# Adding a block-diagonal residual with 64-row matmuls in pairs instead of 128-row matmuls

## The chip, the cores and the metric

The kernel runs on 1 core of one Trainium2 chip. The metric is the device time of one execution in microseconds (us). The five engines are named as the profile names them: PE is TensorE (PE for its matmuls, PEld for its weight loads), DVE is VectorE, ACT is ScalarE, POOL is GpSimd and SP is SyncE.

## What is computed

Attention packs 576 tokens into 32 (`p` attends to `k` and `v`), the tokens then read from the packed ones (`q` attends to the packed result), and a mixer follows: a low-rank mix over tokens, a residual `u`, and a two-layer network with a second residual.

```
p_packed = sm_attn(p, k, v)                  # 8 batches, 8 heads of 64 columns
x        = sm_attn(q, p_packed, p_packed)    # heads side by side: [8, 576, 512]
h = x.T @ U @ V                              # low rank, over tokens
u = x + h.T
out = u + relu(u @ w_ch1) @ w_ch2            # 512 -> 2048 -> 512
```

## The kernel before

`x` is never formed. It is a matrix of attention weights times the packed values, so `u` of one batch is also a matrix of adjusted weights (256 packed rows per token) times a block-diagonal matrix of packed values. The kernel keeps the adjusted weights, transposed, as two parts `ah` and `al` (high and low half of the number, each in fp32r): 128 partitions, two groups `g` of 4 heads, and 576 tokens. In a group the 128 partitions hold 4 heads of 32 packed rows each. The block-diagonal values are `rh` and `rl` (the trace calls both batches' tiles `rdh` and `rdl`): 128 partitions, two groups, 4 heads, 64 columns. Partition block x of group g has values only in the columns of head `x ^ g`, and zeros elsewhere. A product of two split numbers is three matmuls, `mm3` (lines 86 to 88): high by high, high by low, low by high.

A batch goes through 16 steps `kt`, each of 128 of the 2048 hidden columns. `gemm1(kt)` makes hidden columns in two halves of 320 and 256 tokens into `h_ps`, ACT and DVE apply the relu and split the result into `hh` and `hl`, and `gemm2(kt - 1)` of the step before adds 128x512 products into four open accumulators `o[0..3]`, one for each 128 tokens, one PSUM bank each. The remaining 64 tokens of a batch are handled for two batches together by `joint`, which also uses `residual`. Between `gemm1` and `gemm2`, and behind `gemm2`, stand single steps of the next batch's attention (`steps`) and, where `kt % 4 == 2`, `fold`, which multiplies packed values by the first layer's weights. The order of the instructions is the order of this loop, written out by hand.

At `kt == 1` `blocks` fills `rh` and `rl` for the batch. At `kt == 3` `add_u` adds the residual to the four open accumulators: for each token tile t and each group g, `mm3` with a 128x128 stationary tile of `ah` or `al` and 256 moving columns of `rh` or `rl`. This is 4 x 2 x 3 = 24 matmuls in a batch.

```
        def add_u(self):
            for t in range(4):
                c0 = 5 * I * (t // 2) + P * (t % 2)
                ts_ = slice(c0, c0 + P)
                residual(self.o[t], self.ah[:, :, ts_], self.al[:, :, ts_], self.rh, self.rl)
```

Other lines that the trace names: line 229 is `scores` (64x32 stationary tiles at eight places of the array), line 361 is `fold` (64x32 as well), line 304 is `mix1` (128x128 stationary, 256 fp32r columns, and for the last 64 tokens 64x128), lines 318 and 321 are `mix2` (fp32r, 256 and 64 columns).

Of the kernel before, what the change touches and what calls it, by code (L numbers as in the profile page):

```python
# [19 lines left out]
def packed_attention_mixer_kernel(  # L20
# [27 lines left out]
    nc = tc.nc  # L48
# [5 lines left out]
    P = 128  # L54
    SM = 512
    NT = 9
    I = S // NT
# [26 lines left out]
    def mm3(ps, lhs, rhs, start, stop):  # L84
        (lh, ll), (rh, rl) = lhs, rhs
        nc.tensor.matmul(ps, lhsT=lh, rhs=rh, start=start, stop=False)  # L86
        nc.tensor.matmul(ps, lhsT=lh, rhs=rl, start=False, stop=False)  # L87
        nc.tensor.matmul(ps, lhsT=ll, rhs=rh, start=False, stop=stop)  # L88
# [27 lines left out]
    def w2_tiles(pool, n):  # L116
        for i in range(n, n + 2):
            w2t[i] = tuple(pool.tile([P, 4, DM], F32R, name=f"w2{x}{i}", tag=f"w2{x}{i}", bufs=1) for x in "hl")
# [30 lines left out]
    def load_w2(kt):  # L149
        b = bits["w2", kt] = bits_tile()  # L150
        nc.sync.dma_start(out=b.rearrange("p x t -> p (x t)"), in_=w2[kt * P:(kt + 1) * P, :])

    def convert_w2(kt):
        return kt, float32_of(conv_tile(I32), conv_tile(F32), bits.pop(("w2", kt)))

    def split_w2(kt, x):
        hi, lo = w2_parts(kt)
        nc.scalar.copy(hi, x)
        nc.gpsimd.tensor_tensor(lo, x, hi.bitcast(F32), op=ALU.subtract)
# [196 lines left out]
    def fold(b, c):  # L356
        f_ps = [bank() for _ in range(2)]
        for h in range(H):
            g, z = h // 4, h % 2
            xs, zs = slice(32 * (h % 4 ^ g), 32 * (h % 4 ^ g) + 32), slice(64 * z, 64 * z + 64)  # L360
            nc.tensor.matmul(f_ps[g][xs], lhsT=ppT[b][zs, g, xs], rhs=w1t[h // 2][zs, QW * c:QW * c + QW],  # L361
                             start=True, stop=True)
        for a in range(2):
            hi, lo = (pipe.tile([P, 2, QW // 2], F32R, name=f"wt{x}", tag=f"wt{x}", bufs=3) for x in "hl")
            cs = slice(QW // 2 * a, QW // 2 * a + QW // 2)
            for g in range(2):
                nc.scalar.copy(hi[:, g], f_ps[g][:, cs])  # L367
                nc.vector.tensor_tensor(lo[:, g], f_ps[g][:, cs], hi[:, g].bitcast(F32), op=ALU.subtract)  # L368
            wt[b, 2 * c + a] = hi, lo
# [192 lines left out]
    class Batch:  # L562
# [44 lines left out]
                ts_ = slice(t * P, t * P + P)  # L607
                mm3(self.o[t], (hh[:, ts_], hl[:, ts_]), w2_parts(kt), kt == 0, kt == NK - 1)

        def add_u(self):  # L610
            for t in range(4):
                c0 = 5 * I * (t // 2) + P * (t % 2)
                ts_ = slice(c0, c0 + P)
                residual(self.o[t], self.ah[:, :, ts_], self.al[:, :, ts_], self.rh, self.rl)

        def store(self):
            for j in range(2):
# [8 lines left out]
    def residual(ot, xh, xl, rh, rl):  # L626
        for g in range(2):
            mm3(ot[:, g * 256:(g + 1) * 256], (xh[:, g], xl[:, g]), (rh[:, g], rl[:, g]), False, False)

    def joint_parts(b, n):  # L630

        hi, lo = conv_tile(F32R), conv_tile(F32R)
        k0 = 4 * n
        for (dst, src) in ((slice(0, 1), jslot(b, k0)), (slice(1, 4), k0 + 1)):
            w = dst.stop - dst.start
            src = hj[:, src:src + w].rearrange("p k x -> p (k x)")
            cs = slice(P * dst.start, P * dst.stop)
            nc.scalar.copy(hi[:, cs], src)
            nc.vector.tensor_tensor(lo[:, cs], src, hi[:, cs].bitcast(F32), op=ALU.subtract)
        return hi, lo  # L640

    def joint(b, parts):

        oj = psO.tile([P, DM], F32, name="o", tag="o")
        for kt in range(NK):
            if kt % 4 == 0:
                hi, lo = parts.pop(0)
                if kt // 4 + 2 < NK // 4:
                    parts.append(joint_parts(b, kt // 4 + 2))
            cs = slice(P * (kt % 4), P * (kt % 4) + P)  # L650
            mm3(oj, (hi[:, cs], lo[:, cs]), w2_parts(kt), kt == 0, kt == NK - 1)
            if kt == 0:
                for i in range(2):
                    residual(oj, ajh[i], ajl[i], rdh[i], rdl[i])
        return oj

    def store_joint(b, oj):
        os_ = conv_tile(F32)
        nc.scalar.copy(os_, oj)
        for i in range(2):  # L660
            nc.sync.dma_start(out=out[b - 1 + i].rearrange("(i c) m -> c i m", c=NT)[8], in_=os_[I * i:I * i + I])

    w2x = convert_w2(1)
    last, parts = None, []
    for b in range(B):
        cur = Batch(b)
        oj = None
        ahead = attention(b + 2, res) if b + 2 < B else []
        for kt in range(NK):
            cur.gemm1(kt)  # L670
            if oj and kt == 1:
                store_joint(b - 1, oj)
            if rest:
                rest.pop(0)()
            elif steps and (b == 0 or kt % 4 != 2):
                steps.pop(0)()
            if (b, kt) == (0, 5):
                w2_tiles(ctx.enter_context(tc.tile_pool(name="sC", bufs=1, side="right", reuse_waits="tile")), 2)
            if kt > 0:
                cur.gemm2(kt - 1)  # L680
            elif last:
                last.gemm2(NK - 1)
                last.store()
                if last.b % 2 == 1:
                    oj = joint(last.b, parts)
            if w2x:
                split_w2(*w2x)
                w2x = None
                if kt + 3 < NK:
                    load_w2(kt + 3)  # L690
                if kt + 2 < NK:
                    w2x = convert_w2(kt + 2)
            if kt % 4 == 2 and (b, kt) != (B - 1, NK - 2):
                n = b * NPC + kt // 4 + 1
                fold(n // NPC, n % NPC)
            elif steps:
                steps.pop(0)()
            if kt == 1:
                cur.blocks()
            if kt == 3:  # L700
                cur.add_u()
            if ahead and kt == 13:
                ahead.pop(0)()
            if kt == NK - 1 and b % 2 == 1:
                parts = [joint_parts(b, 0), joint_parts(b, 1)]
        assert not steps
        steps = ahead
        last = cur
# [35 lines left out]
```

## Time and profile before

| | us |
|---|---|
| median of 3 runs | 881.36 (880.0 to 882.8) |
| profiled execution, its own time | 877.17 |
| profiled execution, span from first to last instruction | 875.2 |
| PE busy | 836.0 (96% of the span) |
| PE weight loads busy | 665.1 (76%) |
| DVE busy | 402.6 (46%) |
| ACT busy | 322.8 (37%) |

The first 122 us pack the tokens. From there the eight batches follow each other. The mean granted clock of TensorE over the span is 0.973 of full speed. A row of the view of instructions in order of time gives the start, the recorded duration and the instruction. Recorded durations of matmuls overlap, since they are pipelined: what a matmul costs in a dense stream is the distance from its start to the start of the next one.

### The profile page before, as it was taken

What the parts mean: (1) busy time and instruction counts of PE and PEld (TensorE: products, weight loads), DVE (VectorE), ACT (ScalarE), POOL (GpSimd) and SP (SyncE); (2) the same over time, 40 slices, a digit from 0 to 9 for tenths busy, and PEclk for the clock granted to TensorE, in tenths of its full rate; (3) what the DMA queues carried; (4) which work ended last, traced back from release to release, by engine and by line L of the source; (5) the groups of instructions that cost most, each with busy time, mean ns of one, the idle gap of its engine ahead of it and who ended that gap; (6) DMA issues with size and microseconds to landing.
All of it is one profiled execution on the core that took longest, in us unless ns stands there. A gap on an engine that the chain in (4) does not pass through costs nothing.

```text
span 875.2 us, 14665 instructions
## 1 busy us (share of the span) xinstructions
PE 836.0 (96%) x5808; PEld 665.1 (76%) x5808; DVE 402.6 (46%) x988; ACT 322.8 (37%) x1000; POOL 95.0 (11%) x111
## 2 busy tenths in 40 slices
PE   5878899979999999999999999999999999999997
PEld 2554557858888888788878878888888887888886
DVE  4699757876433323433443433434343334332221
ACT  3666564534322333234223332233223332332221
POOL 0002222323001100100010000110011001010000
PEclk8799799989999999999999999999999999999999
DMA  8999833322100110011001100011001100010001
GB/s 273 290 337 292 278 115 102 95 75 85 49 1 1 61 53 10 1 61 49 1 1 61 49 13 1 1 61 49 1 1 61 48 13 1 1 49 1 1 1 60
DMA packets 38979, 59.08 MB, mean 68 GB/s; under 512 B 11776, under 2 KB 21888, under 8 KB 38912
## 3 DMA queue, kind: packets, MB, share of 16 engines
q1 hardware_dynamic: 38912, 58.16, 20.4%
q8 instruction: 45, 0.74, 0.4%
q14 instruction: 22, 0.18, 0.1%
HBM read 47.79 MB, written 10.35 MB: 66 GB/s over the span
## 4 chain that ended last, share of the span: by engine, by line
PE 85%; DVE 7%; DMA 4%; issue 1%; ACT 1%; POOL 0%; SPq 0%; ACTq 0%; DVEq 0%; POOLq 0%
PE o L86 16%; PE o L88 16%; PE o L87 16%; PE h_ps L86 8%; PE h_ps L88 7%; PE h_ps L87 7%; PE t_ps L361 4%; DMA bits<-in_moe_w_ch_dram 2%; PE t_ps L208 1%; DVE os L80 1%; PE t_ps L229 1%; PE s_ps L229 1%; PE t_ps L304 1%; PE t_ps L236 1%; DMA x<-in_moe_U_dram 1%
## 5 line engine op out<-in xcount | busy, mean ns | idle before, releaser
L86 PE MATMUL o<-w2h,hh 128*128 128x512 f32 x512 | 208.7, 408 | 0.0
L88 PE MATMUL o<-w2h,hl 128*128 128x512 f32 x512 | 203.5, 397 | 0.0
L87 PE MATMUL o<-w2l,hh 128*128 128x512 f32 x512 | 203.0, 397 | 0.0
L599 DVE SCALAR_TENSOR_TENSOR hl<-h_ps,hh 128x256 fp32r<-128x256 f32 x256 | 104.4, 422 | 167.2 <-ACT hj L598 154.4
L596 ACT ACTIVATE hh<-h_ps 128x256 fp32r<-128x256 f32 x256 | 98.9, 388 | 188.9 <-PE h_ps L88 188.1
L86 PE MATMUL h_ps<-ah,wth 128*128 128x320 f32 (+1 forms) x512 | 158.2, 309 | 1.2 <-DVE hl L599 1.2
L87 PE MATMUL h_ps<-al,wth 128*128 128x320 f32 (+1 forms) x512 | 151.6, 296 | 0.0
L88 PE MATMUL h_ps<-ah,wtl 128*128 128x320 f32 (+1 forms) x512 | 151.4, 296 | 0.0
L86 PEld LDWEIGHTS h_ps<-ah,wth 128*128 128x128 f32 x512 | 96.9, 189 | 32.7 <-issue 25.7
L88 PEld LDWEIGHTS o<-w2h,hl 128*128 128x128 f32 x512 | 97.1, 190 | 23.1
L86 PEld LDWEIGHTS o<-w2h,hh 128*128 128x128 f32 x512 | 97.4, 190 | 22.2 <-issue 4.1
L87 PEld LDWEIGHTS o<-w2l,hh 128*128 128x128 f32 x512 | 97.6, 191 | 17.4
L87 PEld LDWEIGHTS h_ps<-al,wth 128*128 128x128 f32 x512 | 97.0, 189 | 1.9
L88 PEld LDWEIGHTS h_ps<-ah,wtl 128*128 128x128 f32 x512 | 97.0, 190 | 0.0
L368 DVE TENSOR_TENSOR wtl<-t_ps,wth 128x256 fp32r<-128x256 f32 x128 | 48.5, 419 | 93.9 <-ACT wth L367 90.5
L367 ACT CAST wth<-t_ps 128x256 fp32r<-128x256 f32 x128 | 43.4, 374 | 109.1 <-PE t_ps L361 97.1
L324 POOL TENSOR_TENSOR al<-aT,ah 128x320 fp32r<-128x320 f32 (+1 forms) x32 | 26.2, 818 | 211.6 <-ACT ah L323 211.6
L268 POOL TENSOR_TENSOR e<-e,m 128x576 f32<-128x576 f32 x16 | 19.6, 1226 | 237.8 <-DVE m L267 232.4
L361 PE MATMUL t_ps<-w1t,ppT 64*32 64x512 f32 x512 | 36.5, 601 | 0.0
L323 ACT CAST ah<-aT 128x320 fp32r<-128x320 f32 (+1 forms) x32 | 13.9, 433 | 52.8 <-DVE aT L322 52.8
L279 POOL TENSOR_TENSOR e<-e,s 128x576 f32<-128x576 f32 x16 | 18.9, 1179 | 110.3 <-DVE s L278 106.4
L296 DVE TENSOR_TENSOR x<-t_ps,x 128x512 fp32r<-128x512 f32 (+1 forms) x24 | 14.3, 599 | 32.6 <-ACT x L295 32.6
(130 smaller groups left out, 1021.9 us busy)
## 6 DMA issues: line engine op xcount, KB each, us to landing
bits<-in_moe_w_ch_dram SPq DMA_DIRECT2D x32, 512.0 KB, 4.9
kx<-in_k_dram SPq DMA_DIRECT2D x16, 576.0 KB, 6.1
x<-in_q_dram SPq DMA_DIRECT2D x16, 576.0 KB, 4.8
vt<-in_v_dram SPq DMA_DIRECT2D x64, 128.0 KB, 4.9
out_dram<-bits SPq DMA_DIRECT2D x32, 256.0 KB, 2.4
pn<-in_p_dram SPq DMA_DIRECT2D x16, 64.0 KB, 5.6
vt<-in_v_dram SPq DMA_DIRECT2D x16, 64.0 KB, 4.2
out_dram<-os SPq DMA_DIRECT2D x8, 128.0 KB, 2.3
```

The source lines that it names most:

```text
L86: nc.tensor.matmul(ps, lhsT=lh, rhs=rh, start=start, stop=False)
L87: nc.tensor.matmul(ps, lhsT=lh, rhs=rl, start=False, stop=False)
L88: nc.tensor.matmul(ps, lhsT=ll, rhs=rh, start=False, stop=stop)
L229: nc.tensor.matmul(ss[r][hs, :n], lhsT=lT[rs, g, hs], rhs=t[rs, h, :n], start=True, stop=True)
L268: nc.gpsimd.tensor_tensor(e, e, m.unsqueeze(2).to_broadcast([P, S // 32, 32]), op=ALU.subtract)
L279: nc.gpsimd.tensor_tensor(e, e, s.unsqueeze(2).to_broadcast([P, S // 32, 32]), op=ALU.mult)
L324: nc.gpsimd.tensor_tensor(al[:, g, ns], aT[:, ns], ah[:, g, ns].bitcast(F32), op=ALU.subtract)
L361: nc.tensor.matmul(f_ps[g][xs], lhsT=ppT[b][zs, g, xs], rhs=w1t[h // 2][zs, QW * c:QW * c + QW], start=True, stop=True)
L367: nc.scalar.copy(hi[:, g], f_ps[g][:, cs])
L368: nc.vector.tensor_tensor(lo[:, g], f_ps[g][:, cs], hi[:, g].bitcast(F32), op=ALU.subtract)
L596: nc.scalar.activation(hh[:, ms], src, AF.Relu)
L599: nc.vector.scalar_tensor_tensor(hl[:, ms], src, 0.0, hh[:, ms].bitcast(F32), op0=ALU.max, op1=ALU.subtract)
```

## The change

`add_u` takes an argument `odd` and is called twice for each batch, at `kt == 3` with False and at `kt == 5` with True. A call treats one half of the 128 partitions (`z`: rows 0 to 63 or 64 to 127, two heads of a group) for each accumulator. Only the 128 columns of these two heads are computed, since the others are zero for these rows. The matmuls of two accumulators that use different halves stand alternately in the queue. A call has 2 x 2 x 2 x 3 = 24 matmuls with 64x128 stationary tiles and 128 columns, and a batch has 48. `joint` keeps the old form.

```
--- before.py
+++ after.py
@@ -607,11 +607,21 @@
-        def add_u(self):
-            for t in range(4):
-                c0 = 5 * I * (t // 2) + P * (t % 2)
-                ts_ = slice(c0, c0 + P)
-                residual(self.o[t], self.ah[:, :, ts_], self.al[:, :, ts_], self.rh, self.rl)
+        def add_u(self, odd):
+
+            for j in range(2):
+                for g in range(2):
+                    parts = []
+                    for t in (j, 2 + j):
+                        z = (t // 2 + odd) % 2
+                        zs, c0 = slice(64 * z, 64 * z + 64), 5 * I * (t // 2) + P * (t % 2)
+                        cs = slice(256 * g + P * z, 256 * g + P * z + P)
+                        lh, ll = (a[zs, g, c0:c0 + P] for a in (self.ah, self.al))
+                        rh, rl = (x[zs, g, 2 * z:2 * z + 2].rearrange("p h d -> p (h d)") for x in (self.rh, self.rl))
+                        parts.append((self.o[t][:, cs], ((lh, rh), (lh, rl), (ll, rh))))
+                    for n in range(3):
+                        for o, terms in parts:
+                            nc.tensor.matmul(o, lhsT=terms[n][0], rhs=terms[n][1], start=False, stop=False)
@@ -697,8 +707,8 @@
-            if kt == 3:
-                cur.add_u()
+            if kt in (3, 5):
+                cur.add_u(kt == 5)
```

## Rows read from the trace of the kernel before

**Rows 1.** The page, part 1: busy us, share, instructions of the engine.

```profile
PE 836.0 (96%) x5808; PEld 665.1 (76%) x5808; DVE 402.6 (46%) x988; ACT 322.8 (37%) x1000; POOL 95.0 (11%) x111
```

**Rows 2.** Busy time in stretches: PE, PEld, DVE, ACT, POOL, then clock, DMA.

```profile
200.00:872.30 672.30, 668.76 (x4120) 549.96 (x4118) 253.62 (x622) 213.79 (x677) 54.17 (x55) 1.00 0.08 26
...
184.00:190.50 6.50, 1.90 (x13) 1.72 (x14) 5.59 (x13) 2.02 (x8) 2.40 (x2) 0.94 0.27 85
190.50:196.60 6.10, 6.10 (x18) 4.82 (x19) 4.42 (x8) 2.06 (x5) 1.28 (x1) 0.51 0.21 81
```

**Rows 3.** PE in order of time (start, duration): `add_u` of one batch and its neighbours.

```profile
240.41 0.36 PE L86 MATMUL o<-rdh,ah 128*128 128x256 f32 x1
240.61 0.28 PE L87 MATMUL o<-rdl,ah 128*128 128x256 f32 x1
240.73 0.28 PE L88 MATMUL o<-rdh,al 128*128 128x256 f32 x1
...
243.25 0.28 PE L88 MATMUL o<-rdh,al 128*128 128x256 f32 x1
243.37 0.31 PE L86 MATMUL h_ps<-ah,wth 128*128 128x320 f32 x1
243.52 0.31 PE L87 MATMUL h_ps<-al,wth 128*128 128x320 f32 x1
```

**Rows 4.** PE and its weight loads in order of time, around the 64-row matmuls of line 304.

```profile
202.36 0.28 PE L304 MATMUL t_ps<-x,ua 128*128 128x256 f32 x1
202.57 0.38 PE L304 MATMUL t_ps<-x,ua 64*128 64x256 f32 x1
202.79 0.28 PE L304 MATMUL t_ps<-x,ua 64*128 64x256 f32 x1
202.57 0.18 PEld L304 LDWEIGHTS t_ps<-x,ua 64*128 64x128 f32 x1
202.68 0.19 PEld L304 LDWEIGHTS t_ps<-x,ua 64*128 64x128 f32 x1
203.00 0.42 PE L86 MATMUL h_ps<-ah,wth 128*128 128x320 f32 x1
203.25 0.31 PE L87 MATMUL h_ps<-al,wth 128*128 128x320 f32 x1
203.40 0.31 PE L88 MATMUL h_ps<-ah,wtl 128*128 128x320 f32 x1
```

**Rows 5.** Line 229 in 149.2 to 150.0, its own view, and PE around it.

```profile
L229 PEld LDWEIGHTS t_ps<-xT,ppT x16: 103/104/106, 149.3 to 149.4; 64*32 64x32 f32 x16
L229 PE MATMUL t_ps<-xT,ppT x16: 376/414/453, 149.3 to 149.6; 64*32 64x320 f32 x8, 64*32 64x256 f32 x8
...
149.32 0.76 PE L229 MATMUL t_ps<-xT,ppT 64*32 64x320 f32 x16
150.01 0.51 PE L86 MATMUL o<-w2h,hh 128*128 128x512 f32 x1
```

**Rows 6.** PE and its weight loads in order of time, around the narrow matmul of line 321.

```profile
204.91 0.24 PE L321 MATMUL t_ps<-vs,ms 128*128 128x64 f32 x1
204.97 0.47 PE L86 MATMUL o<-w2h,hh 128*128 128x512 f32 x1
205.28 0.40 PE L87 MATMUL o<-w2l,hh 128*128 128x512 f32 x1
205.51 0.40 PE L88 MATMUL o<-w2h,hl 128*128 128x512 f32 x1
204.91 0.21 PEld L86 LDWEIGHTS o<-w2h,hh 128*128 128x128 f32 x1
205.04 0.19 PEld L87 LDWEIGHTS o<-w2l,hh 128*128 128x128 f32 x1
```

**Rows 7.** The chain that ended last, in the first batch (start, us, what).

```profile
162.87 1.02 PE t_ps L361 x16
...
189.89 0.43 DVE wtl L368
190.46 1.08 PE t_ps L236 x4
191.55 0.43 PE o L86
```

## The prediction

> **What bounds the kernel now.** I read the page's busy times first. PE is busy for 96% of the span, and its weight loads for 76% [rows 1]. This is an average, so the stretches come next: from 200 us to the end of the dense part PE is busy for 668.76 of 672.30 us, at full granted clock, while DVE has 253.62 and ACT 213.79 [rows 2]. In seven of the eight batches PE hardly ever waits, and a microsecond added to its queue is a microsecond added to the end. Only the first batch differs. Its chain leaves PE after 162.87 us and runs through DVE and others up to 190.46 [rows 7]. PE is idle for 4.6 of the 6.5 us from 184 to 190.5, and in the 6.1 us behind that the granted clock is 0.51, the lower of its two levels [rows 2].
>
> A recorded matmul duration is of no use for a price here, because matmuls overlap: the 128x256 ones last 0.28 us and start 0.12 us apart. So I price from start to start. The old residual runs from 240.41 (its first) to 243.25 (its 24th), and the next instruction follows at 243.37 [rows 3]. Its price in a dense stream is 24 x 0.12 = 2.88 us for a batch, 23.0 us for eight.
>
> **What is removed and added.** The 24 matmuls of 256 columns go, and with them 2.88 us. In their place come 2 rounds of 24 matmuls, 12 pairs each, of 64x128 weights and 128 columns. If both matmuls of a pair run together, the columns that pass one after the other fall from 24 x 256 to 24 x 128, half. Two things could eat that gain, and the trace shows both.
>
> The first is entering and leaving the 64-row form. Line 304 does this with fp32r operands and weights of the same shape, 64x128 [rows 4]. Its last 128-row matmul starts at 202.36 and the first 64-row one at 202.57, 0.21 later in place of 0.12: 0.09 lost. That first one is followed after 0.22, so 0.10 more: its weight load was not hidden. Its recorded duration is 0.38 against 0.28 for the second, the same 0.10. From the last 64-row matmul to the next 128-row one are 0.21, and that one is followed after 0.25 in place of the 0.15 that its 320 columns take: a second load that nothing hides, 0.10. The change's last matmul has 128 columns in place of 256, half of the 0.107 that 256 columns take at full clock (2.4 GHz, one column a cycle), so I take 0.16 for the 0.21. A round thus has 0.09 + 0.10 + 0.16 + 0.10 = 0.45 us, whatever its pairs cost, and a batch has two rounds.
>
> The second is the spacing p of the pairs; between 12 pairs there are 11. The round costs 0.45 + 11p. Before does not show a pair of this form, so I bound p by the nearest rows.
>
> - Do the halves of the array work side by side? Line 229 says so for 64x32 weights: 16 matmuls of 376 to 453 ns each need 0.76 us together, and all 16 weight loads start between 149.3 and 149.4 [rows 5]. Eight places are in use there, two row halves by four column blocks.
> - Does a half load its next weights while it multiplies? The second load of line 304 starts at 202.68, while the first matmul has its 256 columns still to pass, and the second matmul has no load time in its duration [rows 4]. So yes.
> - How long is a load? 202.57 to 202.68, so 0.11 us [rows 4]; 64 rows load no faster than 128. A matmul of 128 columns passes in about 0.05, so the pair is limited by its loads and not by its columns. Lower end of p: 0.11.
> - Upper end: the one place where a short fp32r matmul leaves a load uncovered is line 321 with 64 columns. From its start to the next matmul's follower are 205.28 - 204.91 = 0.37 us; 0.23 of these belong to the 512-column matmul between (205.28 to 205.51), so 0.14 are left for 64 columns, and the weight load beside it takes from 204.91 to 205.04 [rows 6]. Upper end of p: 0.14.
>
> I take p = 0.12, between these ends and equal to the spacing of the same operands today [rows 3]. A round is then 0.45 + 1.32 = 1.77 us, two are 3.54, and a batch gets 3.54 - 2.88 = +0.66 us. Eight batches: +5.3 us. With p = 0.11 the sum is +3.5, with 0.14 it is +8.8. In words: the halved columns bring nothing, since 128 columns no longer cover a weight load, there are twice as many loads, which pairwise just make up for it, and two trips into the 64-row form are paid on top. The trips alone count 16 x 0.45 = 7.2 us.
>
> A rule of the Trainium skill would make it worse. TensorE: Matmul & The Clock Gate, in its part on packing small matmuls, says that a weight load overlaps a running matmul only if the two use different row groups. By it each half would alternate between load and matmul. The trace does not agree, as the second load of line 304 shows [rows 4]; what it would cost here is the second rival.
>
> **Where the work moves.** Half of the residual moves from the end of step 3 to the end of step 5, ahead of `gemm1(6)`. No DMA and no wait moves with it: `rh` and `rl` are written in step 1, the four accumulators stay open up to step 15, and nothing else is released by `add_u`. Step 3 gets 1.1 us shorter, step 5 gets 1.77 longer. Behind the second round the relu and the split of `h_ps` on ACT and DVE wait that much longer; both have the time, being busy for less than 40% [rows 2]. Were that cover gone, `gemm2` of the step would wait for `hl`, up to the same 1.77 us. In the first batch DVE is the tighter engine, and the standstill before 190.46 [rows 7] may swallow up to this batch's 0.66; I leave it in the sum. The other edits, slices and flags, cost nothing: they add no instruction beside the matmuls and their loads.
>
> **The rivals.**
>
> 1. *Faster: the loads don't limit, the columns do.* Then p is 0.053 + 0.013 = 0.066 (128 columns, and the 0.013 by which 0.12 exceeds 256 columns), a round is 1.18, a batch 2.35 against 2.88, and the end comes 4.2 us earlier: 877 us. It decides from p = 0.09 down, where two rounds cost 2.88. For it speaks only that I never saw two halves load 128 columns each; against it, that a single half's load takes 0.11 [rows 4]. The Trainium skill's TensorEngine Tiling, section Theoretical Speedup, promises up to twice the speed for a contraction of 64 or fewer; that is this rival, and no 64x128 pair in the trace can test it.
> 2. *No load under a matmul of the same half.* p = 0.11 + 0.05 + 0.01 = 0.17, a round 2.32, a batch +1.76, all +14: 895 us. Against it stands the load at 202.68 [rows 4].
> 3. *The halves don't run side by side in this form.* All four column blocks of a half are in use at once, unlike in line 229, where each place had 32 weights [rows 5]. 23 spacings of 0.11 make a round 2.98 and a batch +3.1: +25, 906 us. The same size results if narrow fp32r operands pass slowly, as the 0.14 for 64 columns could also be read [rows 6]: 0.28 for 128, +33, 915 us. Matmuls of lines 229 and 361, which do overlap, speak against the first reading.
> 4. *No measurable change.* The stall of the first batch is shortened, the clock is not lowered behind it, and this gives back the price. The twelve 512-column matmuls of a `gemm2` at 0.43 in place of 0.23 [rows 6, 7] cost 2.4 us there. +5.3 - 0.7 - 2.4 = +2.2: 883.6 us. For it: PE arrives at the stall later by 0.66. Against it: 4.6 us without work [rows 2] would still be 3.9.
>
> **How the numbers follow.** The sum is made on the profiled execution, which took 877.17 us with a span of 875.2, about 4 us less than the median 881.36 of the runs shown (880.0 to 882.8). An added 5.3 us is the same on either, so the forecast is 881.36 + 5.3 = 886.7 us. Chances: this case 0.60, with its own range 884 to 891; rival 1 0.08; rival 2 0.08; rival 3 0.14; rival 4 0.10. The range 877 to 897 takes in all but rival 3 and half of the outer cases. About 0.3% (2.6 us) is what a measurement of this kernel can tell from no change. Faster gets 0.09 (rival 1 and a little of rival 4), the same 0.14 (the rest of rival 4 and the low end of my own case), slower 0.77.
>
> **What would show it.** In the changed kernel 384 matmuls of 64x128 by 128 columns; pairs starting together, then a distance of 0.11 to 0.14 between pairs (rival 1: under 0.09; rival 2: 0.17; rival 3: single matmuls 0.11 apart or more); a gap of 0.09 more than usual ahead of each of 16 rounds, and an uncovered load of 0.10 at either end; 1.77 us a round. Elsewhere the distances of PE's starts must not change, and DVE's and ACT's idle time after step 5 must not show up as a wait of PE. I am wrong above all if p is not what line 304's single half lets me expect, or if the first batch's stall and its clock shift by microseconds.

## The result and the profile after

The changed kernel takes 883.32 us (median of 15 runs, 879.41 to 885.91), the kernel before 879.96 (15 runs beside them, 876.04 to 882.8). The ratio is 1.0038, 95% interval 1.0022 to 1.0053: slower by 3.3 us (1.9 to 4.7). Forecast was slower by 5.3 (0.66 us a batch). The direction, the place and the cause are those forecast; the size is not.

The second round of a batch, PE in order of time (start, duration), to be held against [rows 3]:

```profile
252.66 0.39 PE L88 MATMUL o<-w2h,hl 128*128 128x512 f32 x1
252.98 0.33 PE L624 MATMUL o<-rdh,ah 64*128 64x128 f32 x2
253.15 0.27 PE L624 MATMUL o<-rdl,ah 64*128 64x128 f32 x2
253.26 0.27 PE L624 MATMUL o<-rdh,al 64*128 64x128 f32 x2
...
254.15 0.28 PE L624 MATMUL o<-rdl,ah 64*128 64x128 f32 x2
254.27 0.28 PE L624 MATMUL o<-rdh,al 64*128 64x128 f32 x2
254.47 0.41 PE L86 MATMUL h_ps<-ah,wth 128*128 128x320 f32 x1
254.72 0.31 PE L87 MATMUL h_ps<-al,wth 128*128 128x320 f32 x1
```

Each row is a pair (x2), and two matmuls of 0.27 us together still last 0.27: the two halves of the array do work side by side. But pairs start 0.11 apart, not 0.055. The round is entered 0.32 after a 512-column matmul in place of 0.23 (0.09 lost); it takes 1.285 us from its first matmul to its last; its last one is followed after 0.20, and that one after 0.25 in place of 0.15 (0.10 lost). These are 1.68 us a round, 3.36 a batch, against 2.88 before: +0.48.

The weight loads of the same kernel show what sets the 0.11:

```profile
252.98 0.19 PEld L624 LDWEIGHTS o<-rdh,ah 64*128 64x128 f32 x2 [0.36 <-issue]
253.09 0.19 PEld L624 LDWEIGHTS o<-rdl,ah 64*128 64x128 f32 x2
253.20 0.19 PEld L624 LDWEIGHTS o<-rdh,al 64*128 64x128 f32 x2
253.31 0.19 PEld L624 LDWEIGHTS o<-rdh,ah 64*128 64x128 f32 x2
```

They run in pairs too, each pair 0.11 behind the one before, and the matmuls follow at their pace. That the loads set this pace, and not the matmuls, is shown by the experiments on the spacing.

The stretches of the kernel after, as in [rows 2] (PE, PEld, DVE, ACT, POOL, clock, DMA):

```profile
200.00:876.90 676.90, 673.34 (x4294) 550.13 (x4292) 254.80 (x625) 215.05 (x680) 54.30 (x55) 1.00 0.08 27
...
184.00:190.90 6.90, 2.83 (x28) 1.72 (x25) 6.05 (x13) 1.71 (x4) 2.41 (x2) 1.00 0.21 76
190.90:197.70 6.80, 5.81 (x16) 4.77 (x17) 5.29 (x10) 3.06 (x8) 1.28 (x1) 0.50 0.22 77
```

PE is as tightly filled as before, and DVE and ACT have the same work (253.62 and 213.79 before). The first batch keeps its standstill, 4.1 us, and the lower clock behind it.

To see where in the kernel the time goes, I take the distance from the first `h_ps` matmul of a batch to that of the next, in the trace of each kernel. Batches alternate between two lengths, since every second one has a joint tile.

| kernel | first batch | batch 2 | batch 3 |
|---|---|---|---|
| before | 96.95 | 86.85 | 99.40 |
| after | 97.21 | 87.30 | 99.84 |
| rows128_two_rounds | 97.04 | 86.87 | 99.39 |
| four_trips | 97.11 | 88.01 | 100.53 |
| wide | 97.39 | 87.64 | 100.16 |
| halves_in_turn | 98.21 | 89.18 | 101.70 |
| half_weights | 95.06 | 86.07 | 98.59 |
| rows128_half_columns | 95.23 | 86.67 | 99.20 |
| no_residual | 93.88 | 83.97 | 96.49 |
| beside | 95.24 | 86.24 | 98.77 |
| rows128_behind_fold | 95.40 | 86.35 | 98.92 |
| rows128_behind_folds | 94.61 | 85.77 | 98.29 |

Over all eight batches the kernel after is longer by 0.26, then 0.44 to 0.50 seven times: 3.5 us, the measured 3.3. The two spans differ by 4.6 us (879.8 and 875.2); the other 1.1 lie ahead of the first batch, in code that is the same. Ahead of it the profiled executions of these kernels differ by nearly 8 us, so single spans are not compared below.

First batches have to be compared with care as well. In the six kernels halves_in_turn, half_weights, rows128_half_columns, beside, rows128_behind_fold and rows128_behind_folds the clock behind the standstill is back at its full level sooner than in the other six. The 6.8 us from the fall of the clock on have a mean granted clock of 0.75 in half_weights, against 0.50 in the kernel after (above):

```profile
189.30:196.10 6.80, 6.80 (x33) 5.91 (x33) 5.03 (x9) 3.06 (x8) 1.28 (x1) 0.75 0.21 77
```

Step 11, which holds the standstill, takes 10.6 to 10.9 us in these six and 11.6 to 12.1 in the others, so about 1 us of a difference between first batches can be the clock. What decides it is not shown. Batches 2 and 3 run at the full clock in all of them.

### The profile page after: what moved, and what is told of

Same layout as the page of the kernel before. It is cut to its first block, busy times and chain, and to the rows that moved or that the text cites. A ratio compares the mean times of both kernels' runs of the same rounds, so it can differ in the third digit from the quotient of the medians.

```text
span 879.8 us, 15049 instructions
## 1 busy us (share of the span) xinstructions
PE 838.4 (95%) x6000; PEld 664.3 (76%) x6000; DVE 402.4 (46%) x988; ACT 322.3 (37%) x1000; POOL 95.1 (11%) x111
## 4 chain that ended last, share of the span: by engine, by line
PE 86%; DVE 6%; DMA 4%; issue 1%; ACT 1%; SPq 1%; POOL 0%; DVEq 0%; POOLq 0%; ACTq 0%
PE o L86 15%; PE o L88 15%; PE o L87 15%; PE h_ps L86 9%; PE h_ps L88 7%; PE h_ps L87 7%; PE t_ps L361 4%; DMA bits<-in_moe_w_ch_dram 3%; PE o L624 3%; PE t_ps L208 2%; DMA kx<-in_k_dram 2%; PE t_ps L229 1%; PE s_ps L229 1%; PE t_ps L304 1%; DVE os L80 1%
## 5 line engine op out<-in xcount | busy, mean ns | idle before, releaser
L88 PE MATMUL o<-w2h,hl 128*128 128x512 f32 x512 | 203.3, 397 | 0.0
L88 PE MATMUL h_ps<-ah,wtl 128*128 128x320 f32 (+1 forms) x512 | 151.4, 296 | 0.0
L88 PEld LDWEIGHTS o<-w2h,hl 128*128 128x128 f32 x512 | 97.1, 190 | 23.0
L88 PEld LDWEIGHTS h_ps<-ah,wtl 128*128 128x128 f32 x512 | 97.0, 189 | 0.0
L268 POOL TENSOR_TENSOR e<-e,m 128x576 f32<-128x576 f32 x16 | 19.6, 1227 | 249.5 <-DVE m L267 241.7
L208 PE MATMUL k_ps<-ident,kx 128*128 128x128 f32 x128 | 25.4, 352 | 4.6 <-DMA kx<-in_k_dram 4.2
```

The source lines that it names most:

```text
L208: nc.tensor.transpose(t_ps[:, o:o + P], x[:, h, P * j:P * j + P], ident)
L268: nc.gpsimd.tensor_tensor(e, e, m.unsqueeze(2).to_broadcast([P, S // 32, 32]), op=ALU.subtract)
```

## Experiments

Every ratio is to the kernel before, run on the same chip; the interval is at 95%. 0.0011 of a ratio is 1 us. The changed kernel stands at 1.0038.

**Is it the move?** (rows128_two_rounds)

```
-        def add_u(self):
-            for t in range(4):
+        def add_u(self, ts):
+            for t in ts:
...
-            if kt == 3:
-                cur.add_u()
+            if kt in (3, 5):
+                cur.add_u((0, 1) if kt == 3 else (2, 3))
```

> The old 128-row matmuls, 12 at step 3 (accumulators 0 and 1) and 12 at step 5 (accumulators 2 and 3): only the place is changed. Theory A (the loss is the trips into the 64-row form plus a pair spacing set by the weight load; the move is free): no change against before, within 1 us, and 24 matmuls 0.12 us apart in each batch. Rival B (moving half of the residual to step 5 makes other engines late): about +3 us, and the time of step 5 grows by more than 12 x 0.12 = 1.44 us.

Measured: 0.9995 (0.998 to 1.001), and batches 2 and 3 as before within 0.02 us. Splitting the old residual over two steps costs nothing. Rival B falls.

**Is it the trips?** (four_trips: each round cut in two, at steps 3, 4, 5 and 7)

```
-        def add_u(self, odd):
+        def add_u(self, odd, js):
...
-            for j in range(2):
+            for j in js:
...
-            if kt in (3, 5):
-                cur.add_u(kt == 5)
+            if kt in (3, 4, 5, 7):
+                cur.add_u(kt in (5, 7), (int(kt in (4, 7)),))      # second argument: the j of this round
```

> The changed kernel with each round of 12 pairs cut into two of 6 pairs, at steps 3, 4, 5 and 7: twice the trips, the same matmuls. Theory A: a trip has 0.46 us that its pairs don't explain and one spacing fewer, so 16 more trips cost 16 x (0.46 - 0.11) = 5.6 us, about +9 us against before. Rival E (the loss lies in the pairs, and entering and leaving costs next to nothing in a real queue): it stays near +3.4 us.

Measured: 1.008 (1.0063 to 1.0096), +7.0 us (5.5 to 8.4). The expected +9 lies a little outside. By the trace batches 2 and 3 have +0.71 and +0.69 us over the kernel after, as the sum says (2 x 0.35 = 0.70), but the first batch has nothing more (97.11 against 97.21). There PE waits for DVE's `hl` at the start of step 11, and this wait is shorter by 1.0 us, in the kernel after and then in four_trips:

```profile
186.20 0.41 PE L86 MATMUL h_ps<-ah,wth 128*128 128x320 f32 x1 [1.23 <-DVE hl L599]
```

```profile
187.66 0.42 PE L86 MATMUL h_ps<-ah,wth 128*128 128x320 f32 x1 [0.23 <-DVE hl L599]
```

Rival E falls: sixteen more trips cost close to what was forecast of each, where PE is the limit.

**Is the spacing the load?** Three kernels. wide has twice the columns for the same loads:

```
-                        cs = slice(256 * g + P * z, 256 * g + P * z + P)
+                        cs = slice(256 * g, 256 * g + 256)
-                        rh, rl = (x[zs, g, 2 * z:2 * z + 2].rearrange("p h d -> p (h d)") for x in (self.rh, self.rl))
+                        rh, rl = (x[zs, g].rearrange("p h d -> p (h d)") for x in (self.rh, self.rl))
```

> The changed kernel with 256 moving columns in each 64-row matmul, where the added 128 columns are zeros of the block-diagonal values. Theory A (the pair spacing of 0.111 us is the weight load, and half of the time in which it runs no column passes): doubled columns hide under the load, the spacing becomes the 0.12 of the 128-row form, a round grows by 11 x 0.009 + 0.05 = 0.15 us, 16 rounds by 2.4 us: about +5.8 us against before. Rival C (a pair costs its columns plus a fixed part): the spacing becomes 0.111 + 0.053 = 0.164, 16 rounds grow by 10 us: about +13.6 us against before.

Measured: 1.006 (1.0042 to 1.0079), +5.3 us (3.7 to 6.9). PE in order of time, kernel wide:

```profile
255.97 0.39 PE L624 MATMUL o<-rdh,ah 64*128 64x256 f32 x2
256.19 0.28 PE L624 MATMUL o<-rdl,ah 64*128 64x256 f32 x2
256.31 0.28 PE L624 MATMUL o<-rdh,al 64*128 64x256 f32 x2
256.43 0.28 PE L624 MATMUL o<-rdh,ah 64*128 64x256 f32 x2
256.55 0.28 PE L624 MATMUL o<-rdl,ah 64*128 64x256 f32 x2
```

0.12 between pairs: twice the columns for 0.01 us. Only the first pair, whose load nothing hides, is followed later than in the kernel after, 0.22 in place of 0.165.

half_weights has half the load for the same columns:

```
-                        lh, ll = (a[zs, g, c0:c0 + P] for a in (self.ah, self.al))
+                        lh, ll = (a[zs, g, c0:c0 + 64] for a in (self.ah, self.al))
-                        parts.append((self.o[t][:, cs], ...
+                        parts.append((self.o[t][:64, cs], ...
```

> The changed kernel with 64 in place of 128 weight columns in each 64-row matmul, so that only the first 64 tokens of each accumulator get their residual (the other half of it is left out); the 128 moving columns stay. Theory A (the weight load sets the spacing): a load of half the columns takes half the time, the spacing falls from 0.111 to about 0.06 us, 16 rounds lose 16 x 11 x 0.05 = 9 us: about -5.5 us against before. Rival C (the columns, the issue or the write into PSUM set it): the spacing stays, about +3.4 us.

Measured: 0.9896 (0.9874 to 0.9919), -9.2 us (-11.1 to -7.1), more than expected. PE in order of time:

```profile
336.72 0.28 PE L624 MATMUL o<-rdh,ah 64*64 64x128 f32 x2
336.83 0.22 PE L624 MATMUL o<-rdl,ah 64*64 64x128 f32 x2
336.89 0.22 PE L624 MATMUL o<-rdh,al 64*64 64x128 f32 x2
336.95 0.22 PE L624 MATMUL o<-rdh,ah 64*64 64x128 f32 x2
337.01 0.22 PE L624 MATMUL o<-rdl,ah 64*64 64x128 f32 x2
```

0.06 between pairs. The same 128 columns pass twice as often once the load is half as long. The kernel also writes half as many rows of the result, but writing can't be what sets the pace: wide writes twice the columns for 0.01 us. Batches 2 and 3 are 1.2 us shorter than those of the kernel after. The first is 2.2 shorter, and 1.1 of it is step 11 (10.88 against 11.95), where the clock is back sooner. All eight batches together are 7.4 us shorter than before; the rest of the 9.2 is not seen in them, and lies within the interval.

rows128_half_columns is the old form with half the columns:

```
-                residual(self.o[t], self.ah[:, :, ts_], self.al[:, :, ts_], self.rh, self.rl)
+                for g in range(2):
+                    mm3(self.o[t][:, g * 256:g * 256 + P], (self.ah[:, g, ts_], self.al[:, g, ts_]),
+                        tuple(x[:, g, :2].rearrange("p h d -> p (h d)") for x in (self.rh, self.rl)), False, False)
```

> The kernel before, with 128 in place of 256 moving columns in each of the 24 matmuls of a batch (the residual of two heads in each group is left out). Theory A: the weight load alone holds the spacing at about 0.11, so halving the columns of the old form gives 24 x 0.01 x 8 = 2 us, about -2 us. Rival C (columns set it): the spacing falls to 0.067, 24 x 0.053 x 8 = -10 us.

Measured: 1.0001 (0.9979 to 1.0023). The interval still holds -2 us and excludes -10; batches 2 and 3 are shorter by 0.18 and 0.20, where 24 x 0.01 are 0.24. PE in order of time:

```profile
339.55 0.28 PE L88 MATMUL o<-rdh,al 128*128 128x128 f32 x1
339.66 0.27 PE L86 MATMUL o<-rdh,ah 128*128 128x128 f32 x1
339.77 0.27 PE L87 MATMUL o<-rdl,ah 128*128 128x128 f32 x1
```

0.11 again. The old form had its 256 columns for almost the price of the load: passing half of them saves 0.2 us a batch. All three runs speak against rival C.

**Does the alternating order matter?** (halves_in_turn)

```
+            odd = int(odd)
...
-            for j in range(2):
-                for g in range(2):
+            for z in range(2):
+                for j, g in ((0, 0), (0, 1), (1, 0), (1, 1)):
                     parts = []
-                    for t in (j, 2 + j):
-                        z = (t // 2 + odd) % 2
+                    for t in (j + 2 * (z ^ odd),):
```

> The same 24 matmuls of a round, but all 12 of rows 0 to 63 first and then all 12 of rows 64 to 127, so that no two neighbours use different halves. Theory A (each half loads and multiplies on its own, and alternating order lets both do so at once): 23 spacings of 0.111 and the trip, 3.0 us a round in place of 1.68, +2.6 us a batch over the changed kernel, about +25 us against before. Rival D (the spacing is a price of issuing instructions, 0.055 each, or PE reorders them by itself): the order doesn't matter, and it stays near +3.4 us.

Measured: 1.0204 (1.0185 to 1.0223), +18.0 us (16.3 to 19.6). Most of the expected loss is there, so the order counts and rival D falls; but a round takes 2.23 us from first to last matmul, where 23 x 0.11 are 2.53. PE in order of time, at the change from one half to the other:

```profile
258.26 0.27 PE L624 MATMUL o<-rdl,ah 64*128 64x128 f32 x1
258.37 0.27 PE L624 MATMUL o<-rdh,al 64*128 64x128 f32 x1
258.38 0.38 PE L624 MATMUL o<-rdh,ah 64*128 64x128 f32 x2
258.55 0.33 PE L624 MATMUL o<-rdl,ah 64*128 64x128 f32 x2
258.66 0.32 PE L624 MATMUL o<-rdh,al 64*128 64x128 f32 x2
258.77 0.27 PE L624 MATMUL o<-rdh,ah 64*128 64x128 f32 x1
```

The first half has 12 matmuls, four times (rdh,ah), (rdl,ah), (rdh,al). At 258.38 its ninth has just started, three are left, and a second matmul of the same kind (x2) begins beside the tenth. PE starts the other half's first matmuls ahead of three that stand before them in the queue.

**What is the residual worth?** (no_residual: both calls removed)

> The kernel without the calls of add_u (the residual of the four accumulators is left out, that of the joint tile stays). Theory A: it is worth what its 24 matmuls take from start to start, 2.88 us a batch, -23 us against before, and less in the first batch if that one's stall gives some of it back: -20 to -23. Rival F (other engines' waits behind it are part of its price): more than 24 us.

Measured: 0.9752 (0.9726 to 0.9778), -21.8 us (-24.1 to -19.5). Batches 2 and 3 are 2.88 and 2.91 shorter. The price of 24 x 0.12 holds, and nothing else hangs on it. Rival F would need more than 24 us, just at the end of the interval, but the batches leave no room for it.

**Can the trips be shared?** (beside)

```
+    def step(batch):                     # in place of steps.pop(0)()
+        s = steps.pop(0)
+        s()
+        if s.__name__ == "mix1":
+            batch.add_u(True)
...
-            if kt in (3, 5):
-                cur.add_u(kt == 5)
+            if kt == 6:                  # behind the fold of this step
+                cur.add_u(False)
+            if kt == 13 and b == B - 1:  # the last batch has no mix1
+                cur.add_u(True)
```

> The changed kernel with its two rounds placed beside 64-row work that is there anyway: the first directly behind the fold of step 6, the second directly behind the two 64x128 matmuls of line 304 at step 12 (in the last batch, which has none, at step 13). Theory A: the second round's trip is already paid, 0.46 - 0.11 = 0.35 us in seven batches, and the first saves one entry, 0.09 us in eight: -3.2 us against the changed kernel, within 1 us of before. Rival G (each change of tile shape drains PE, whatever stood before): nothing saved at the fold, -2.5 us; Rival H (nothing is saved at either place): +3.4 us against before.

Measured: 0.995 (0.9926 to 0.9973), -4.4 us, where about 0 was expected: faster than both kernels. Two parts of the surplus are seen in order of time. At step 12, in this kernel:

```profile
286.33 0.95 PE L304 MATMUL t_ps<-x,ua 128*128 128x256 f32 x5
286.90 0.32 PE L624 MATMUL o<-rdh,ah 64*128 64x128 f32 x1
287.06 0.27 PE L624 MATMUL o<-rdl,ah 64*128 64x128 f32 x1
287.12 0.28 PE L304 MATMUL t_ps<-x,ua 64*128 64x256 f32 x1
...
288.41 0.27 PE L624 MATMUL o<-rdh,al 64*128 64x128 f32 x1
288.61 0.50 PE L86 MATMUL o<-w2h,hh 128*128 128x512 f32 x1
```

The residual of the other half runs beside line 304's two matmuls, which stood alone before [rows 4], and step 12 grows by 1.28 us. Behind the fold a round adds 1.48: the fold's own way back to 128 rows is used for the way into the round (from the fold's start to the next instruction are 1.02 us in either case, 354.98 to 356.00 here and 257.27 to 258.29 in the kernel before). That is 2.76 in place of 3.36. The rest, 0.5 us a batch, is in step 7: 5.35 us against 5.85 before (from its first `h_ps` matmul to that of step 8, in the fourth batch), with none of the residual in it. My sum had no term for that.

**What is in step 7?** (rows128_behind_fold, rows128_behind_folds: the old 128-row code in another place, where `add_u` takes the list of its accumulators)

```
-            if kt == 3:
-                cur.add_u()
+            if kt in {6: (0, 1, 2, 3)}:                             # rows128_behind_fold
+                cur.add_u({6: (0, 1, 2, 3)}[kt])
...
+            if kt in {6: (0, 1), 10: (2,), 14: (3,)}:               # rows128_behind_folds
+                cur.add_u({6: (0, 1), 10: (2,), 14: (3,)}[kt])
```

> The old 24 matmuls of 128 rows, unchanged, but placed behind the fold of step 6 in place of the end of step 3. The 64-row rounds beside the fold and line 304 gained more than their trips: step 7 went from 5.85 to 5.35 us. Theory J (the scores of step 7 need the two banks that the fold of step 6 has just filled, and wait until they are copied out; work put in between fills the wait): the old form gains the same 0.5 us a batch, -3 to -4 us against before, and about as much as the kernel with the rounds beside. Rival K (the gain of that kernel is the 64-row form itself, shared trips alone): no change against before, step 7 stays 5.85.

Measured: 0.9963 (0.9949 to 0.9978), -3.3 us (-4.5 to -1.9), step 7 takes 5.26 us. Theory J holds and rival K falls.

> The old 24 matmuls of 128 rows, 12 behind the fold of step 6, 6 behind that of step 10 and 6 behind that of step 14. Theory J: the steps behind these folds (7, 11, 15) each start with a PE wait on a bank of the fold, 0.5, 0.25 and 0.25 us; 1.44, 0.72 and 0.72 us of matmuls in between fill all three, about 1 us a batch in those that have the next batch's attention steps: -6 to -8 us against before, faster than all kernels so far. Rival L (the 0.25 us of steps 11 and 15 are no bank wait but go with the change of instruction): -3 to -4 us, as with the whole residual behind step 6.

Measured: 0.9909 (0.9894 to 0.9925), -8.0 us (-9.3 to -6.6), 871.0 us: the fastest of all. Steps 7, 11 and 15 take 5.26, 4.98 and 4.63 us in place of 5.85, 5.35 and 5.05; 0.1 of each difference is the uncovered load behind the fold, which now falls into the step of the fold, the rest is the wait. Batches 2 to 7 are each 1.07 to 1.11 us shorter than before, 6.6 us together, and the last one is as before. The first is 2.34 shorter, with about 1 us of it in the clock. Rival L falls.

In the kernel before, line 229 of step 7 waits twice (its own view and the DVE rows next to it):

```profile
L229 PEldq EVENT_SEMAPHORE  x2: 51/51/51, 260.1 to 260.5; - x2
...
258.81 1.62 DVE L368 TENSOR_TENSOR wtl<-t_ps,wth 128x256 fp32r<-128x256 f32 x4 [3.38 <-ACT wth L367]
```

DVE's copies out of the fold's two banks last until 260.43, the second wait of the scores ends behind 260.5, and the scores use the same two banks (`psT`, bufs=2). Idle time of the weight loads from 200 to 872 us (count, busy, mean ns, idle), before and then in rows128_behind_folds:

```profile
L236 PEld LDWEIGHTS t_ps<-ident,aT 128*128 128x128 f32 x48 | 5.5, 141 | 2.4 <-PE h_ps L88 1.6
L318 PEld LDWEIGHTS t_ps<-vs,ms 128*128 128x128 f32 x28 | 5.3, 189 | 2.2 <-PE h_ps L88 1.6
L229 PEld LDWEIGHTS t_ps<-xT,ppT 64*32 64x32 f32 x192 | 3.1, 104 | 4.9 <-issue 2.2 <-PE h_ps L88 1.6 <-ACT rdh L577 1.1
```

```profile
L236 PEld LDWEIGHTS t_ps<-ident,aT 128*128 128x128 f32 x48 | 5.8, 141 | 0.8
L318 PEld LDWEIGHTS t_ps<-vs,ms 128*128 128x128 f32 x28 | 5.3, 191 | 0.6
L229 PEld LDWEIGHTS t_ps<-xT,ppT 64*32 64x32 f32 x192 | 2.2, 104 | 3.0 <-issue 1.1 <-ACT rdh L577 1.1
```

The waits were named "PE h_ps L88", which is no cause but the last thing that PE did. Behind the copies they disappear.

## Why the prediction was right and wrong

**The step that failed is "I take p = 0.12": the spacing of the pairs was mis-sized.** It measured 0.112, next to the lower of the two ends, which a row of the same shape had shown directly (the loads at 202.57 and 202.68 [rows 4]). The 0.12 was taken as the spacing of the same operands today, but that spacing has 256 columns in it: with 128 columns the old form stands at 0.11 too (rows128_half_columns). Line 321's 0.14 [rows 6], the upper end, is from a place of another kind (128 rows, 64 strided columns); why it needs 0.14 was not tested. The difference of 0.008 in 11 spacings of 16 rounds is 1.4 of the 2.0 us by which the change was forecast too high. The lower end of the sum, +3.5, was the right one.

Two more terms of the round were wrong, and nearly cancel. The uncovered first load was put at 0.10 and is 0.05: the first spacing is 0.165 where line 304 has 0.22, since 128 columns pass behind the load and not 256 (wide, with 256, has 0.22 as well). The way out was put at 0.16 and is 0.20: half the columns don't shorten it, as wide leaves after 0.21. A round is thus 1.68 instead of 1.77. That these two errors cancel was luck.

The forecast time, 886.7, is 3.4 us above the measured 883.32. 2.0 of this is the change; the other 1.4 is the base, the median of 3 runs at 881.36, where 15 runs gave 879.96.

**The first batch.** I left its full 0.66 in the sum, though its chain leaves PE. In the two traces it is 0.26: steps 3 to 7 grow by 0.48, as in other batches, step 11 with the standstill is 0.12 shorter and step 0 is 0.09 shorter. Sixteen more trips don't lengthen it at all, as the wait for `hl` gives them back. These are single executions, and 0.2 us is little beside what the clock does there.

**Confirmed.** The halves work side by side (rival 3 falls: halves_in_turn is what it would have cost, less the overlap at the seam). Loads run under the matmuls of their own half (rival 2 falls: p is 0.11, not 0.17). Columns don't set the pace (rival 1 falls: half_weights reaches 0.06 only with half the load). The price of the old residual, 2.88 us a batch, holds (no_residual), the move is free (rows128_two_rounds), and entering costs the 0.09 and the second uncovered load the 0.10 that line 304 shows. Rival 4 falls: the standstill is still 4.1 us long and the clock is 0.50 behind it.

**What I didn't see.** I looked for work that hides the residual, not for waits that the residual could hide. Three waits of a batch, 1.1 us together, stood in the trace of before behind the folds, in each of batches 2 to 7. Both kernels put the residual where PE has no gap; the place is worth more than the form: -8.0 us with the old form against +3.3 with the new. The new form behind all three folds was not tried.

## What to carry to other kernels

Price a matmul in a dense stream by the longer of its weight load and its columns; here the load of 128 weight columns was 0.11 us. Cutting columns below the load brought nothing, and more tiles with the same weight columns mean more loads; halve the load and see whether the spacing follows. Work without deadlines, such as an addition to an open accumulator, belongs behind a matmul whose bank must be copied out before the next one can start; and each further trip into the 64-row form cost 0.35 us here, unless it stood beside one that was there anyway.

## What the runs showed of the hardware

- PE starts matmuls of one half of the array ahead of others that stand before them in its queue: three of them in halves_in_turn, and in beside the first residual of one half starts at 286.90, with line 304's second matmul following only at 287.12. The Trainium skill's TensorE: Matmul & The Clock Gate, in its part on packing small matmuls, says that matmuls start in strict order; the rows show otherwise for two halves.
- Weight loads of 64 rows by 128 columns follow each other after 0.11 us, as those of 128 rows do (rows128_half_columns); with 64 columns it is 0.06 (half_weights). Two halves load at the same time without slowing each other: 0.11 in pairs, and 0.11 for one half alone in halves_in_turn.
- Spans ahead of the first batch, in unchanged code, differed by nearly 8 us between profiled executions (121.8 to 129.6 us to the first `h_ps` matmul), more than the change itself.
- After the same idle time of PE in step 11 (3.83 us) the lower clock did not last equally long: in the 6.8 us from its fall on the mean granted clock was 0.50 in the kernel after and 0.75 in half_weights, and step 11 took 11.95 and 10.88 us.
